# Attention feeding a gated projection, one core: q and k of batches 2 to 7 turned on TensorE instead of by DMA transposes

## The chip, the cores and the metric

The kernel runs on one core of a Trainium2 chip. The metric is the device time of one launch in microseconds (us). Engines are named as in the profile: PE is TensorE (PEld its weight loads), DVE is VectorE, ACT is ScalarE, POOL is GpSimd, and SP is SyncE, which here only issues DMAs.

## What is computed

Attention with a squared ReLU in place of the softmax, for 8 batches of 12 heads, 448 positions and a head size of 64. Then a two-layer projection with a quick GELU:

```python
scores = (1.0 / np.sqrt(D)) * np.matmul(q, k.transpose(0, 1, 3, 2))   # q, k, v: 8, 12, 448, 64
attn = np.maximum(scores, 0.0) ** 2 / S                               # S = 448
x = np.matmul(attn, v).transpose(0, 2, 1, 3).reshape(B * S, H * D)    # 3584, 768
h = x @ w_in                                                          # w_in: 768, 2048
out = (h * (1.0 / (1.0 + np.exp(-1.702 * h)))) @ w_out                # w_out: 2048, 768
```

Inputs and output are float32 in DRAM. The kernel computes in float16 with float32 sums.

## The kernel before, in words

**Units.** The attention is cut into 24 units, three per batch. A unit holds four heads of one batch. Its q (and likewise k and v) is viewed by `quad` (L90) as a tile of 128 partitions, each with two blocks of 448 numbers: a block is one head's seven neighbouring positions times 64. The two blocks on a partition belong to two heads, a = 0 and 1; the two halves of the partitions hold two further heads.

**From DRAM to turned q and k.** The scores need q and k with the head size along the partitions, so each tile is transposed, in 7 column blocks j. Before the change there are three ways.
- Unit 0: SP loads float32 into a staging tile (`load`, L94, tiles kst and qst), DVE casts to float16 (`cast`, L104), and PE transposes (`trans_pe`, L123).
- Units 1 to 5: POOL issues a DMA that casts on the way (`load_cast`, L99), and PE transposes. `trans_pe` makes 14 matmuls of 64 columns each, for two heads and seven blocks, and writes to one PSUM bank ("tr"). `trans_evac` (L133) copies the bank to the tile qT or kT on DVE or ACT.
- Units 6 to 23 (batches 2 to 7): SP loads float32 into the one staging tile, an engine casts it and puts the two heads' columns of a block side by side (`c.rearrange("p j a d -> p a j d")`, L111), and SP issues a DMA transpose into qT or kT (`trans_dma`, L114). PE has no part in it. POOL makes 23 of these casts, ACT 10 and DVE 3.

**Scores and values.** `scores` (L140) makes, for each unit and block j, four matmuls on quarters of the array (64 by 64) into two banks ("sc"). `relu` (L153) and `square` (L162) make the tile "at" on DVE or ACT. `attn_v` (L170) makes 28 quarter-array matmuls of a unit ("av"), and `xt_evac` (L186) copies them to the float16 tile xb.

**The projection.** For batch 0 the first layer is made directly by `m1` (L208, "ht"). For batches 1 to 7 it is made by `unit_product` (L252, "hx"): one level of a Strassen-Winograd scheme with seven products, whose sums of blocks DVE makes. `unit_gelu` and `m1_gelu` run on ACT, and `unit_widen` or `m1_widen` (L204) turn the result to float16 in the tile `ring`, on POOL or DVE. The second layer goes over pairs of 128-row tiles in the same scheme: `pair_product` ("ox"), sums by `a_sum`, and `pair_snap` and `pair_last`, which bring a product to the output tile osb (L82, L366). `store` (L301) issues the output DMAs from SP. The matmuls of all projections are recorded at L194, copies at L78 to L82 and sums at L85.

**What sets the order.** The order of every engine's work is written out by hand as one list of words (from L428). A word names an operation, its unit or tile, the engine after ":" and the PSUM banks after "@"; `tq6@4` would turn q of unit 6 by way of bank 4, `Rq6` does it by DMA transpose, `eq0:a` evacuates on ACT. `Lq`, `Lk` are staged loads, `jq`, `jk`, `V` are casting loads, `Q`, `K` are casts. Each engine runs its operations in that order and waits on semaphores for data and for free buffers. SP's queue thus holds staged loads, DMA transposes and output stores in one line, and POOL's holds casting loads, casts and widenings. A `sp_gate` (L381) makes SP's loads for batch 2 wait until a block of w_in has landed. Buffers that bear on the change: k16 and q16 have 2 each, kT and qT 3, the staging tiles 1; there are 8 PSUM banks.

At the start, 16 matmuls on zeros ("zp") run on PE before data are there.

Of the kernel before, what the change touches and what calls it, by code (L numbers as in the profile page):

```python
# [8 lines left out]
F32 = mybir.dt.float32  # L9
# [6 lines left out]
def kernel(  # L16
# [31 lines left out]
    for name, bufs in (("cst", 1), ("kst", 1), ("qst", 1), ("k16", 2), ("q16", 2), ("v16", 4),  # L48
                       ("kT", 3), ("qT", 3), ("at", 15), ("xb", 2),
                       ("T1", 1), ("T2", 1), ("T4", 1), ("gf", 5),  # L50
                       ("as0", 1), ("as1", 1), ("osb", 3)):
        pool(name, bufs)
# [10 lines left out]
    gate = const("gate", [1, 64])  # L63
# [30 lines left out]
    def load(n, u):  # L94
        x = new(f"{n}st", [128, 2, S], F32)
        nc.sync.dma_start(out=x, in_=quad(n, u))
        units[u][n + "st"] = x

    def load_cast(n, u):  # L99
        x = new(f"{n}16", [128, 2, S], F16)  # L100
        nc.gpsimd.dma_start(out=x, in_=quad(n, u))
        units[u][n + "16"] = x

    def cast(n, e, u):  # L104
        x = units[u].pop(n + "st")
        if u == 0:
            c = new(f"{n}16", [128, 2, S], F16)
            copy(e, c, x)
        else:
            c = new(f"{n}16", [128, J, 2, D], F16)  # L110
            copy(e, c.rearrange("p j a d -> p a j d"), x.rearrange("p a (j d) -> p a j d", d=D))  # L111
        units[u][n + "16"] = c

    def trans_dma(n, u):  # L114
        t = new(f"{n}T", [128, J, 128], F16)
        nc.sync.dma_start_transpose(
            out=t[:, :, :], in_=units[u].pop(n + "16").rearrange("p j a d -> p (j a d)"))
        units[u][n + "T"] = t
# [4 lines left out]
    def trans_pe(n, p, u):  # L123
        ps = bank(p, "tr", F16)
        x = units[u].pop(n + "16")
        for j in range(J):
            for a in range(2):
                nc.tensor.matmul(  # L128
                    out=ps[64 * a:64 * a + 64, j * 128:(j + 1) * 128],
                    lhsT=x[:, a, 64 * j:64 * j + 64], rhs=ident[:, :], is_transpose=True)  # L130
        units[u][n + "ps"] = ps
# [176 lines left out]
    def store_part(e, p, m, h, i):  # L308
# [3 lines left out]
            NOUT + NOUT // 2 * (h - 2), NOUT + NOUT // 2 * (h - 1))  # L312
# [32 lines left out]
    def pair_product(e, p, m, n, h=None):  # L345
        c = (0, 1, 0, 1, 0, 0, 1)[n] if h is None else 2 + h
        if n < 2 or (n == 3 and h is not None):
            op[m, c] = bank(p, "ox")
# [4 lines left out]
        mm(op[m, c][:, k], lambda f: a[:, f, :], lambda f: w[:, f, k], HF, n in (0, 1, 3))  # L353

    def pair_snap(e, p, m, n):
        i, c = {0: (0, lo), 2: (0, hi), 4: (1, hi)}[n]
        copy(e, out_tile(m + i)[:, c], op[m, 0][:, 0:NOUT], 1.0 / SC)

    def pair_last(e, p, m, n, h=None):
        i, c = {1: (0, lo), 3: (1, hi), 5: (1, lo), 6: (0, hi)}[n]  # L360
        o = out_tile(m + i)[:, c][:, quarter(h)]
        if n == 5:
            copy(e, o, op[m, 0][:, 0:NOUT], 1.0 / SC)
        else:
            x = op[m, 1 if h is None else 2 + h][:, quarter(h)]
            nc.vector.scalar_tensor_tensor(out=o, in0=x, scalar=1.0 / SC, in1=o,  # L366
                                           op0=ALU.mult, op1=ALU.add)
# [13 lines left out]
    def sp_gate(e, p, i):  # L381
        nc.sync.dma_start(out=gate[0:1, :], in_=win[i][127:128, 0, 0:64])

    with tc.manual_schedule():
# [4 lines left out]
               "G": sp_gate,  # L389
# [3 lines left out]
        for n in "kq":  # L393
# [3 lines left out]
            two["R" + n] = lambda e, p, u, n=n: trans_dma(n, u)  # L397
# [22 lines left out]
        def zeros(e, p, n):  # L420
# [8 lines left out]
            "z9@0 z1 z1 jq1 z1 z1 jk1 V1 I Lq0 Lk0 z1 z1 z1 Q0:d tq0@1 eq0:a K0:d tk0@2 tq1@3 ek0 "  # L429
            "eq1 s0.5@4.5 jq2 r0.5.1:d r0.5.0 s0.1@6.7 jk2 s0.2@0.1 r0.2.1 r0.1.1:d jq3 s0.0@2.3 "  # L430
            "s0.3@5.4 r0.1.0 r0.2.0:d r0.3.1 r0.3.0:d s0.4@1.7 tk1@6 ek1 s1.6@0.4 s1.4@5.6 jk3 x0.2 "
            "r0.0.0 V0 r0.4.1 r0.0.1 x0.0 r0.4.0 r1.6.0 s0.6@2.7 x0.3 jwa0 s1.0@3.1 r1.6.1 r1.0.1 "
            "tq2@0 x0.5 eq2 s1.5@4.1 r1.4.1 r1.5.0:d s1.3@0.6 jwb0 r1.4.0 r1.5.1 V2 s1.1@4.5 x1.6 "
            "tk2@1 jq4 r1.3.1 jwb2 x1.4 r0.6.1 ek2 r1.1.1 x0.4 jk4 r0.6.0 jwa2 r1.1.0 r1.0.0 tq3@6 "
            "s2.3@7.1 eq3 x0.1 r1.3.0 r2.3.0 s1.2@5.2 r1.2.1 jwa1 x1.1 jwb1 x0.6 tk3@4 r2.3.1 ek3 "
            "jq5 V3 a0@3.6 r1.2.0 jk5 x1.0 jwb3 x1.2 x1.3:a s2.4@0.7 e0.1:a e0.0:a r2.4.0 s3.3@2.1 "
            "x1.5 r3.3.0:d r3.3.1 r2.4.1:d a1@4.5 e1.0:a V4 e1.1:a s2.2@6.3 r2.2.1:d jwa3 s2.5@0.2 "
            "V5 r2.2.0 x2.3 f0.2.0@1 r2.5.0 jo1.0 s2.0@7.4 r2.0.1 s2.1@5.3 r2.1.1 r2.0.0:d r2.5.1 "
            "f0.2.1 jo0.0 x2.2 f0.3.0@6 r2.1.0:d f0.3.1 x2.0 s2.6@0.4 r2.6.1 r2.6.0 s3.1@3.7 r3.1.0 "
            "s3.0@2.5 r3.1.1:d jo1.1 tq4@4 f0.1.0@0 jo0.1 r3.0.0:d eq4 x2.4 x2.6 x2.1:a f0.1.1 "  # L440
            "s3.2@3.7 x2.5:a r3.2.0 a2@2.4 tk4@3 r3.2.1:d r3.0.1 e2.0:a s3.6@7.5 e2.1 ek4 f0.3.2 "
            "r3.6.0:d x3.2 r3.6.1 f0.2.2 g0.3 g0.2 f0.1.2 g0.1 s3.5@2.4 s3.4@3.7 r3.4.0 r3.4.1 "
            "r3.5.0:d s4.4@5.6 r4.4.0:d r4.4.1 v0.2 f0.0.0@1 x3.3 f0.0.1 f0.0.2 f0.8.0@0 g0.0 "
            "s4.5@3.7 r3.5.1:d S0.1 r4.5.0 s4.6@2.5 r4.6.0:d s4.3@6.1 v0.1 f0.8.1 r4.3.0 f0.8.2 "
            "x3.6 r4.6.1 x3.5 x3.0 g0.8 v0.3 s4.2@4.3 r4.2.1 S1.1 s4.1@2.6 r4.2.0 f0.4.0@5 f0.4.1 "
            "f0.5.0@0 f0.4.2 r4.1.0 f0.5.1 x4.6:a x4.2:a G3 v0.8 f0.6.0@3 f0.6.1 r4.3.1:d r4.5.1:d "
            "x3.1 S2.1 f0.6.2 f0.5.2 x4.4 x3.4 f0.7.0@4 g0.6 tq5@2 eq5 S1.2 tk5@1 r4.1.1 g0.4 Lq6 "
            "Lk6 S2.2 ek5:a g0.5 a3@7.3 e3.1:a v0.5 s4.0@2.6 s5.2@5.1 r5.2.1 r4.0.0:d f0.11.0@0 "
            "r4.0.1:d f0.11.1 r5.2.0 f0.11.2 e3.0:a x4.0 x4.5 s5.0@3.1 g0.11 s5.4@2.6 x4.3:a r5.0.1 "
            "s5.5@5.7 f0.7.1 r5.5.1 f0.9.0@0 f0.9.1 f0.9.2 r5.0.0:d f0.7.2 r5.5.0:d s5.3@1.7 r5.4.1 "  # L450
            "x4.1 v0.6 g0.7 a4@3.5 S3.1 s5.1@6.4 r5.3.1 r5.4.0 S2.4 v0.11 v0.7 x5.0:a Q6 r5.3.0:d "
            "s5.6@7.2 S1.3 e4.0 f0.10.0@1 g0.9 S3.2 f0.10.1 v0.9:d r5.6.1 r5.1.1:d u1.2.0@3 S0.3 "
            "f0.15.0@0 x5.3:a f0.14.0@2 r5.1.0 x5.1 f0.15.1 r5.6.0:d v0.4 f0.15.2 f0.14.1 x5.2:a "
            "v0.0 g0.15 f0.10.2 x5.4 T1.1 f0.14.2 u1.3.0@4 g0.10 x5.6:a f0.13.0@6 x5.5 K6 Lk7 "
            "a5@7.0 f0.13.1 S1.4 e4.1:a S3.4 S0.2 S2.3 Lq8 f0.13.2 v0.10:d e5.0:a v0.15:d e5.1:a "
            "Rq6 T1.2 u1.0.0@1 u1.1.0@5 u1.1.1@7 S0.4 t1.0.0 Rk6 g0.14 t1.1.0 T1.3 v0.14:d b1.1.1 "
            "u1.0.2 g0.13 u1.0.1@0 u1.1.2 t1.0.2 u1.0.4 v0.13 b1.0.1 g1.1.1 v1.1.1 W1.1 g1.0.1 "
            "v1.0.1 S3.3 t1.1.2 f0.12.0@2 u1.0.3 t1.0.4 u1.1.4 t1.2.0 T1.4 b1.0.3 u1.1.3 t1.1.4 "
            "u1.3.1@6 g1.0.3 u1.0.6 K7 W2.1 b1.1.3 b1.0.6 u1.0.5 Lk8 f0.12.1 W0.1 v1.0.3 u1.1.6 "
            "u1.2.1@0 g1.0.6 W3.1 b1.1.6 g1.1.3 u1.1.5 b1.2.1 v1.0.6 g1.0.5 u1.2.2 t1.3.0 v1.1.3 "  # L460
            "u1.2.3 g1.2.1 v1.0.5:d v1.2.1 W3.2 t1.2.2 b1.3.1 f0.12.2 W0.2 W0.3 g1.1.6 u1.2.4 g0.12 "
            "p0.0@7 v0.12 t1.2.4 W1.3 Q8:a b1.2.3 v1.1.6 Lq7 u1.2.5 A0.1@0 g1.2.3 W3.3 u1.3.2 Rq8 "
            "A0.2@1 g1.2.5 W2.2 h0.0 u1.2.6 b1.2.6 g1.3.1 v1.3.1 u1.3.3 g1.1.5 W2.4 W1.2 t1.3.2 "
            "p0.1@1 V6 v1.1.5 Rk7 s6.0@2.3 r6.0.0:d A0.3 r6.0.1 v1.2.5 s6.1@0.5 r6.1.0 l0.1 u1.3.4 "
            "t1.3.4 r6.1.1 p0.2 A0.4 x6.0:a s6.2@2.3 r6.2.1 h0.2:d r6.2.0:d s6.4@0.5 r6.4.1 p0.3 "
            "W2.3 b1.3.3 Q7:a W0.4 s6.3@3.2 r6.3.1 x6.1 p0.4 W1.4 K8:p r6.4.0 r6.3.0 W3.4 h0.4 "
            "x6.3:a Rq7 Lk9 l0.3 Lq9 x6.4 u1.3.5 s6.5@5.2 s6.6@0.3 r6.6.1 g1.3.5 r6.6.0 x6.2 u1.3.6 "
            "r6.5.1:d p0.5 r6.5.0 b1.3.6 g1.2.6 s7.0@3.4 l0.5 v1.2.6 r7.0.0:d x6.5 r7.0.1 x7.0 "
            "s7.2@0.2 r7.2.1 s7.4@5.6 r7.4.1 p0.6 s7.1@7.3 s7.6@4.2 r7.4.0 V8 V7 v1.3.5 r7.1.0:d "
            "Rk8 x7.4 x6.6:a r7.1.1 a6@6.5 r7.6.0 s7.3@7.3 K9:p l0.6 Q9 r7.6.1 e6.0:a r7.3.0:d "  # L470
            "r7.3.1 s7.5@4.1 r7.5.0 Lk11 e6.1 p2.0@2 x7.6 r7.2.0 Rk9 s8.5@6.7 s8.4@3.4 x7.1 "
            "s8.2@5.0 r7.5.1 r8.5.1 r8.2.1 Rq9 p2.1@1 A2.1@1 s8.1@7.0 r8.2.0:d r8.4.1 r8.4.0 x7.2 "
            "x7.3 r8.5.0 r8.1.0:d K11:p s8.3@5.4 r8.1.1 x7.5:a r8.3.0 Rk11 r8.3.1:d x8.1:a a7@3.6 "
# [151 lines left out]
```

## Time and profile before

| | us |
|---|---|
| median of 3 runs | 362.71 |
| lowest and highest | 362.51, 363.19 |
| profiled execution, its own time | 363.36 |
| span of its instructions | 361.6 |
| PE, DVE, ACT, POOL busy | 351.8, 313.2, 286.0, 116.9 |

The span is the time from the first to the last instruction in the profile. An engine's busy time is the part of it in which one of its instructions was running. In a row of the profile, "out<-in" names the tile written and those read, "xN" is the number of instructions, and a number such as L194 is the line of the kernel. In the chain of waits each piece has its start, its length and what it was.

### The profile page before, as it was taken

The numbers are of one execution on the slowest core, as the hardware profiler recorded it, in microseconds if no ns is written. First come the engines' busy times: TensorE is split into PE (matmuls) and PEld (weight loads), VectorE is DVE, ScalarE is ACT, GpSimd is POOL, SyncE is SP. The second block draws the span as 40 slices with busy tenths as digits, with TensorE's granted clock in tenths as the row PEclk, the third lists the DMA queues.
The fourth block names the chain that finished last, engine by engine and source line by source line (L and its number), as shares of the span: only waits on it lengthen the run. The fifth ranks groups of instructions, "written<-read, shape, count | busy, mean of one in ns | idle before, by whom it ended". The sixth has DMA issues, their size and how long they took to land.

```text
span 361.6 us, 9118 instructions
## 1 busy us (share of the span) xinstructions
PE 351.8 (97%) x3600; PEld 240.6 (67%) x3600; DVE 313.2 (87%) x578; ACT 286.0 (79%) x551; POOL 116.9 (32%) x169
## 2 busy tenths in 40 slices
PE   8799999999999999999999999999999999999995
PEld 4444458854579655896568865698579756778663
DVE  3999999999998899899988898989998898674844
ACT  3999898999988998789997799868987898427410
POOL 5735731435135424242244343254121310102000
PEclk9999999999999999999999999999999999999999
DMA  8999999679889999868699625980381101130314
GB/s 178 159 195 205 217 234 240 126 122 229 189 224 268 210 164 182 204 121 199 145 195 172 198 33 86 210 200 0 68 175 46 44 2 45 45 87 2 87 45 133
DMA packets 65388, 51.39 MB, mean 142 GB/s; under 512 B 35776, under 2 KB 62016, under 8 KB 65344
## 3 DMA queue, kind: packets, MB, share of 16 engines
q1 hardware_dynamic: 48336, 36.32, 43.0%
q0 software_dynamic: 16608, 14.09, 26.7%
q8 instruction: 28, 0.46, 0.5%
q10 hardware_dynamic: 400, 0.39, 0.3%
q14 instruction: 16, 0.13, 0.1%
HBM read 45.61 MB, written 11.01 MB: 157 GB/s over the span
## 4 chain that ended last, share of the span: by engine, by line
PE 85%; DMA 6%; DVE 4%; ACT 2%; POOL 2%; issue 1%; POOLq 0%
PE ox L194 34%; PE hx L194 32%; PE sc L147 8%; PE av L178 7%; DMA k<-in_k_dram 3%; DMA q<-in_q_dram 3%; PE ht L214 3%; PE zp L424 1%; DVE at L85 1%; DVE at L158 1%; POOL ring L204 1%; ACT at L160 1%; ACT gf L201 1%; PE tr L128 0%; DVE asum L85 0%
## 5 line engine op out<-in xcount | busy, mean ns | idle before, releaser
L160 ACT ACTIVATE at<-sc 128x448 f16<-128x448 f32 x214 | 104.9, 582 | 7.3 <-PE sc L147 7.2
L204 POOL TENSOR_SCALAR ring<-gf 128x448 f16<-128x448 f32 x94 | 58.0, 617 | 156.1 <-ACT gf L201 152.7
L194 PE MATMUL ox<-wout,ring 128*128 128x384 f16 (+1 forms) x456 | 80.3, 324 | 0.1
L194 PEld LDWEIGHTS <-ring 128*128 128x128 f16 x568 | 53.7, 98 | 35.9 <-issue 6.1
L158 DVE TENSOR_SCALAR at<-sc 128x448 f16<-128x448 f32 x122 | 72.2, 616 | 3.6 <-PE sc L147 2.7
L194 PEld LDWEIGHTS <-win 128*128 128x128 f16 x672 | 64.0, 98 | 6.6 <-issue 3.0
L85 DVE TENSOR_TENSOR at<-at 128x896 f16<-128x896 f16 x102 | 63.1, 644 | 0.3
L166 ACT ACTIVATE at<-at 128x896 f16<-128x896 f16 x66 | 62.7, 969 | 0.8 <-DVE at L158 0.5
L85 DVE TENSOR_TENSOR gf<-hx,gf 128x448 f32<-128x448 f32 x84 | 51.1, 620 | 10.8 <-PE hx L194 4.9
L201 ACT ACTIVATE gf<-gf 128x448 f32<-128x448 f32 x84 | 46.8, 573 | 15.1 <-DVE gf L85 14.9
L194 PE MATMUL hx<-xb,win 128*128 128x224 f16 x504 | 58.0, 259 | 0.0
L147 PE MATMUL sc<-qT,kT 64*64 64x448 f16 x672 | 49.7, 358 | 2.0 <-DVE kT L80 1.4
L194 PEld LDWEIGHTS <-winS 128*128 128x128 f16 x504 | 48.2, 98 | 2.7 <-issue 1.1
L76 ACT ACTIVATE gf<-hx 128x448 f32<-128x448 f32 x59 | 31.4, 542 | 13.2 <-PE hx L194 9.5
L194 PE MATMUL ox<-wT,asum 128*128 128x384 f16 (+1 forms) x232 | 41.0, 321 | 0.7 <-DVE osb L366 0.5
L194 PE MATMUL hx<-T,winS 128*128 128x224 f16 x336 | 39.7, 259 | 0.0
L178 PE MATMUL av<-at,v 64*64 64x448 f16 x672 | 37.1, 350 | 1.2 <-ACT at L160 0.7
L147 PEld LDWEIGHTS <-kT 64*64 64x64 f16 x672 | 18.0, 105 | 25.9 <-issue 18.8
L194 PEld LDWEIGHTS <-asum 128*128 128x128 f16 x232 | 21.4, 98 | 16.8 <-issue 4.4
L366 DVE SCALAR_TENSOR_TENSOR osb<-ox,osb 128x384 f32<-128x384 f32 (+1 forms) x44 | 23.3, 533 | 8.9 <-PE ox L194 6.9
L178 PEld LDWEIGHTS <-v 64*64 64x64 f16 x672 | 19.8, 106 | 14.0 <-issue 2.8
L80 POOL CAST q<-qst 128x896 f16<-128x896 f32 x13 | 13.4, 1028 | 39.6 <-DMA qT<-q 14.5
(57 smaller groups left out, 363.3 us busy)
## 6 DMA issues: line engine op xcount, KB each, us to landing
out_dram<-osb SPq DMA_DIRECT2D x52, 192.0 KB, 3.4
qst<-in_q_dram SPq DMA_DIRECT2D x19, 448.0 KB, 4.9
kst<-in_k_dram SPq DMA_DIRECT2D x19, 448.0 KB, 4.4
v<-in_v_dram POOLq DMA_DIRECT2D x24, 224.0 KB, 5.7
win<-in_moe_w_in_dram POOLq DMA_DIRECT2D x8, 384.0 KB, 12.3
wout<-in_moe_w_out_dram POOLq DMA_DIRECT2D x4, 768.0 KB, 20.6
q<-in_q_dram POOLq DMA_DIRECT2D x5, 224.0 KB, 5.3
k<-in_k_dram POOLq DMA_DIRECT2D x5, 224.0 KB, 5.9
```

The lines of the kernel that those rows point to most:

```text
L76: nc.scalar.activation(out=o, in_=i, func=AF.Copy)
L80: eng[e].tensor_copy(out=o, in_=i)
L85: eng[e].tensor_tensor(out=o, in0=x, in1=y, op=op)
L147: nc.tensor.matmul(out=sc[a][c, 0:S], lhsT=st["kT"][r, j, c], rhs=st["qT"][r, :, c], start=True, stop=True)
L158: nc.vector.tensor_scalar(out=o, in0=i, scalar1=0.0, scalar2=None, op0=ALU.max)
L160: nc.scalar.activation(out=o, in_=i, func=AF.Relu)
L166: nc.scalar.activation(out=at, in_=at, func=AF.Square)
L178: nc.tensor.matmul(out=av[s][64 * a:64 * a + 64, 0:S], lhsT=v16[r, a, 64 * j:64 * j + 64], rhs=at[r, a, :], start=(j == 0), stop=(j == J - 1))
L194: nc.tensor.matmul(out=o, lhsT=lhs(i), rhs=rhs(i), start=start and i == 0, stop=i == n - 1, skip_group_check=True)
L201: nc.scalar.activation(out=o, in_=i, func=AF.Gelu_apprx_sigmoid, scale=1.0 / SC)
L204: eng[e].tensor_scalar(out=o, in0=i, scalar1=SC, scalar2=1.0, op0=ALU.mult, op1=ALU.mult)
L366: nc.vector.scalar_tensor_tensor(out=o, in0=x, scalar=1.0 / SC, in1=o, op0=ALU.mult, op1=ALU.add)
```

## The change

- `load_cast` gets a second form for q and k of units 6 to 23: two casting DMAs from POOL, one for each head a. Each writes pieces of 64 numbers so that the two heads' columns of a block j lie side by side.
- `trans_pe` gets a second form for tiles laid out so: 7 matmuls of 128 columns on the whole array instead of 14 of 64.
- `trans_dma` and the gate are gone, and `cast` keeps only the side-by-side layout, which unit 0 now has too. Units 6 to 23 have no staged load and no cast on an engine.
- k16 and q16 have 4 buffers each instead of 2. The staging tiles are gone; unit 0 is staged in `ring`, which is unused at that time.
- The second layer's copies to osb may come in another order (`from_bank`): the first to come is copied, the second added. The last pair's halves are cut differently.
- The whole list of words is new. The shares of DVE, ACT and POOL in operations that may run on either are new too.

```diff
-    for name, bufs in (("cst", 1), ("kst", 1), ("qst", 1), ("k16", 2), ("q16", 2), ("v16", 4),
+    for name, bufs in (("cst", 1), ("k16", 4), ("q16", 4), ("v16", 4),
...
     def load(n, u):
-        x = new(f"{n}st", [128, 2, S], F32)
-        nc.sync.dma_start(out=x, in_=quad(n, u))
-        units[u][n + "st"] = x
+        o = "kq".index(n) * 4 * S
+        x = ring.rearrange("p f c -> p (f c)")[:, o:o + 4 * S].bitcast(F32)
+        units[u][n + "st"] = x.rearrange("p (a c) -> p a c", a=2)
+        nc.sync.dma_start(out=units[u][n + "st"], in_=quad(n, u))
 
     def load_cast(n, u):
-        x = new(f"{n}16", [128, 2, S], F16)
-        nc.gpsimd.dma_start(out=x, in_=quad(n, u))
+        if n == "v" or u < 2 * NP:
+            x = new(f"{n}16", [128, 2, S], F16)
+            nc.gpsimd.dma_start(out=x, in_=quad(n, u))
+        else:
+            x = new(f"{n}16", [128, J, 2, D], F16)
+            for a in range(2):
+                nc.gpsimd.dma_start(
+                    out=x[:, :, a, :], in_=quad(n, u)[:, a, :].rearrange("p (j d) -> p j d", d=D))
+            x = x.rearrange("p j a d -> p (j a d)")
         units[u][n + "16"] = x
...
-    def trans_dma(n, u):
-        t = new(f"{n}T", [128, J, 128], F16)
-        nc.sync.dma_start_transpose(
-            out=t[:, :, :], in_=units[u].pop(n + "16").rearrange("p j a d -> p (j a d)"))
-        units[u][n + "T"] = t
...
         for j in range(J):
+            if len(x.shape) == 2:
+                nc.tensor.matmul(out=ps[:, j * 128:(j + 1) * 128],
+                                 lhsT=x[:, j * 128:(j + 1) * 128], rhs=ident[:, :],
+                                 is_transpose=True)
+                continue
             for a in range(2):
...
+    def from_bank(e, x, t, c):
+        o = out_tile(t)[:, c]
+        part_done = (t, c.start) in begun
+        begun.update((t, i) for i in range(c.start, c.stop, NOUT // 2))
+        if part_done:
+            nc.vector.scalar_tensor_tensor(out=o, in0=x, scalar=1.0 / SC, in1=o,
+                                           op0=ALU.mult, op1=ALU.add)
+        else:
+            copy(e, o, x, 1.0 / SC)
...
-    def sp_gate(e, p, i):
-        nc.sync.dma_start(out=gate[0:1, :], in_=win[i][127:128, 0, 0:64])
```

A stretch of the list, for units 17 to 21, before and after:

```diff
-            "x17.0 r18.0.0 K20:p Lq21 s17.5@5.7 r17.5.1 h14.0:d s17.1@3.6 Rq20 A14.2@1 r17.1.0:d "
-            "p12.6 x18.2:a p14.1@0 Rk23 p14.2 Lk22 o13 l12.6 r17.5.0 r17.1.1 x17.1:a x17.4 "
...
+            "r17.3.1 x17.2 r17.3.0 tk23@1 l12.6 p14.1@4 ek23:a x17.3 o12 x18.6:a tq20@5 s18.5@7.2 "
...
+            "p14.2 r18.0.1 e17.0 r18.0.0 e17.1 r18.4.1 s19.4@1.7 T5.1 s19.5@0.2 r19.4.0 tq21@6 T5.3 "
+            "r19.5.0 u5.0.0@5 T5.2 tk20@1 r19.5.1:d t5.0.0 u5.1.0@0 r19.4.1 x19.5 u5.0.1@2 eq21:a "
```

## The prediction

> **What bounds the kernel now.** I read the page's busy shares first, then the windows, then the chain that ended last. On the page TensorE (PE) is busy nearly all the time:
>
> ```profile
> PE 351.8 (97%) x3600; PEld 240.6 (67%) x3600; DVE 313.2 (87%) x578; ACT 286.0 (79%) x551; POOL 116.9 (32%) x169
> PEclk9999999999999999999999999999999999999999
> ```
>
> A busy PE is not a PE at its peak, since the ends of its records are modelled. So I ask what its stream must take. The chain of waits (start, length, what; all in us) gives the rates, a piece ending where the next begins:
>
> ```profile
> 50.52 2.65 PE ht L214 x14
> 54.12 1.45 PE av L178 x28
> 131.93 1.32 PE av L178 x28
> 133.63 6.61 PE ox L194 x40
> 140.24 0.50 PE sc L147 x8
> 157.03 7.01 PE hx L194 x72
> 164.04 0.69 PE sc L147 x12
> 242.32 8.05 PE hx L194 x84
> 338.94 18.25 PE ox L194 x128
> ```
>
> hx takes 8.05/84 = 0.0958 a matmul, ht 2.65/14 = 0.189, av 1.32/28 = 0.047. Twelve sc cost 0.19 more than eight: 0.047 each. Eight at that rate are 0.38 and show 0.50, so going from quarter-array sc to a full-array stream costs about 0.1. The 40 ox before an sc block give (6.61 - 0.1)/40 = 0.163; of the last 128, 32 are 192 columns wide, at 0.083. A transposition at L128 is 14 half-array matmuls:
>
> ```profile
> 17.12 0.58 PE L128 MATMUL tr<-ident,k 128*64 128x128 f16 x14
> L128 PE MATMUL tr<-ident,k x84: 217/219/243, 7.0 to 39.9; 128*64 128x128 f16 x84
> ```
>
> From the timeline's 0.58 I take the last record's 0.219: 0.36 for 13 steps, 0.028 a step, so 0.39 for 14. The records start in pairs, a pair every 0.055: two halves side by side.
>
> The sum over counts from the program: ox 768 x 0.1625 = 124.8, narrow ox 32 x 0.083 = 2.7, hx 1176 x 0.0958 = 112.7, ht 96 x 0.189 = 18.1, sc and av 672 each x 0.047 = 63.2, 12 transpositions 4.7, zp 5.3: **331.5**. The order of instructions changes the array's shape 125 times: 125 x 0.1 = 12.5. PE starts at 1.1, and 4.4 remain after its last matmul starts. These make 349.5 of 361.6; **12.1 are waits of PE**. Most are early. The sixth av block ends at 55.2; the stream up to it is 43.2, plus 34 changes (3.4) and the start of 1.1: 47.7. So 7.5 of the 12.1 lie before 55.2, and only 4.6 behind it. The windows (length, then busy time of each engine, clock, DMA share, GB/s) show why:
>
> ```profile
> 0.00:20.00 20.00, 16.14 (x224) 8.90 (x224) 13.91 (x28) 13.73 (x29) 12.13 (x22) 1.00 0.99 171
> 20.00:40.00 20.00, 19.82 (x238) 9.81 (x230) 19.55 (x38) 18.10 (x37) 11.12 (x13) 1.00 1.25 202
> 180.00:200.00 20.00, 20.00 (x202) 14.52 (x195) 17.18 (x32) 17.11 (x30) 7.52 (x10) 1.00 1.05 180
> 280.00:300.00 20.00, 20.00 (x201) 12.88 (x200) 17.93 (x33) 17.96 (x38) 4.51 (x8) 1.00 0.09 22
> ```
>
> At the start PE waits for first data and for VectorE and ScalarE (DVE, ACT), which turn scores into squares; from about 60 on PE is never free. The DMA share is high in one late window and near nothing in the other, with PE at 20.00 in both: **relieving DMA cannot shorten that stretch**.
>
> **The change, part by part.**
>
> *PE gains work.* 36 DMA transposes become 36 PE transpositions of 7 full-array matmuls; q and k of unit 0 go from 14 half-array to 7 full ones. A full one streams 128 columns, as a half one does, and a pair of halves takes 0.055, so I price 7 at 0.39, the row nearest in kind. 36 x 0.39 = **+14.1**; unit 0 saves nothing. Low end: if a full one took a single half's step, 0.028, 7 cost 0.20 and the sum is +7.1. High end: if the 128-column weight load were not hidden, its record of 0.098 (page, L194) would set the step: 0.69 each, +24.7. For the row: hx steps of 0.0958 already include such a load.
>
> The Trainium skill speaks against my price ("TensorE: Matmul & The Clock Gate", Back-to-back issue gap): a sustained stream of loads and matmuls at 128 columns runs at about 81 ns a matmul. By that the term would be 36 x 7 x 0.081 = 20.4, 6.3 more; no full-array transposition is in this trace, while the half-array pairs, which load as many columns, ran at 55 ns.
>
> *Order.* Shape changes go from 125 to 134: **+0.9**. Products, scores and attention matmuls keep their number.
>
> *DVE and ACT.* 36 evacuations of 128x896 come in, 18 on each:
>
> ```profile
> L80 DVE COPY kT<-tr 128x896 f16<-128x896 f16 x5 | 3.1, 621 | 1.3 <-PE tr L128 1.3
> L76 ACT ACTIVATE kT<-tr 128x896 f16<-128x896 f16 x1 | 0.9, 938 | 0.0
> ```
>
> DVE: 18 x 0.62 = +11.2. The new order also moves to it 14 xb copies (+8.7), 13 widenings from POOL (+5.5), 8 squares (+5.0), 7 osb copies (+3.9) and small ones (+0.4); it gives up 16 relus (-9.5), 4 hx copies (-2.4), 4 casts (-2.5). Net +20, to about 333. ACT: +16.7 of evacuations, +7.8 relus, +2.1 hx copies, against -8.5 casts, -7.6 squares, -7.8 xb, -3.4 osb: about even, 285. Over a span near 375 these are 89% and 76%, as 87% and 79% now. So I cost them at nothing beside PE; the cover is PE's own stream. If it is gone (attention stretches, where DVE is fullest), half of the added 20 on the path would cost up to 10.
>
> *POOL.* 23 casts go (-24.4), 13 widenings (-8.0). 72 DMA issues of 896 pieces come; wout, 1024 pieces, took 0.878 each, so 72 x 0.85 = +61. POOL goes to about 146, 39%: hidden. Widenings and v loads stand behind these issues, and an issue waits until a buffer of q16/k16 is turned; four buffers instead of two, and loads ordered several units ahead, make me cost this at nothing. Uncovered, a widening held up delays the sums and products behind it; as an outer price I keep POOL's longest single wait now, 18.9 (for ACT gf), inside the bounds on waits below.
>
> *SP and DMA.* SP loses 38 loads but for unit 0's two, 36 transposes and the gate; only stores remain, so they can only start earlier. DMA packets:
>
> ```profile
> q1 hardware_dynamic: 48336, 36.32, 43.0%
> q0 software_dynamic: 16608, 14.09, 26.7%
> ```
>
> From the trace's packets by size, the loads through kst and qst (9,728 packets) took 60 us of all 16 engines and the transposes (32,256 of 256 B) 57; both go but for unit 0's two loads. In come 36 x 1792 = 64,512 packets of 128 B written, read from 256 B. Casting packets took 79 ns for 768 B and 98 for 1024 B; along that line 128 B is 30, an estimate, and 64,512 x 30/16 = 121: even. High end: 79 as for 768 B, 318; low end: 18 ns, the transposes' median, 73. I take 30, since the 256 B packets averaged 28.
>
> The Trainium skill warns here too ("DMA: Bandwidth & Descriptors", Why small descriptors are slow): a fixed cost per packet weighs more on small ones, with about 27% lost at 256 B. That would make the 121 some 154, still under the span; no 128 B packet is in this trace.
>
> *What stalls go or stay.* The first 55 us still run units 0 to 5 on PE transposes, with the same relus and squares. More q16/k16 buffers let loads start without waiting for a turn (POOL waited 3.3 and 1.5 for PE tr): perhaps 1 to 2 less. Each new transposition holds a PSUM bank from its first matmul to the end of its evacuation, which only the early stretch knew; 36 of them may add some waits of 0.1 to 0.2, up to 7. I take waits of 11 in all (bounds 5 and 20).
>
> **Sum.** 331.5 + 14.1 + 134 x 0.1 + 5.5 = 364.5 with no wait at all; with 11 the span is 375.5. The profiled execution took 363.36, 1.76 outside its span: 377.3. The shown median, 362.71, is 0.65 below it: **376.6**.
>
> **Rivals.**
> 1. *DMA becomes the bound.* v, weights, stores and the first loads take about 130 us of the 16 engines, and loads must be in by about 320, before the last scores. So small packets may cost up to (320 - 130) x 16/64,512 = 47 ns before they bind. At 65 they need 262: the span is about 392 + 10 at the end, and the time some **400**. For it: the share is over 1 in several windows; against: 28 ns at 256 B. Chance 0.08.
> 2. *The weight load is not hidden in full-array transpositions:* 24.7 instead of 14.1, **387**. For it: nothing else alternates a load with so short a matmul on the full array. Chance 0.08.
> 3. *Faster: the transpositions fit into PE's waits.* Place: the waits of 12.1. Price: 0.20 each (0.028 a matmul), 7.1, and all waits gone: 361.6 + 7.1 + 0.9 - 12.1 = 357.5, time **358.6**. It decides from 36 transpositions and changes under 11.4, that is 0.29 each. Against: 7.5 of the waits are early, where no new transposition is needed yet, and 128 columns have never streamed through all rows and columns in less than hx's rate, 0.055. Chance 0.03; about no change, 0.02.
> 4. *The change doesn't do what it says* (half-array turns remain, 14 per tile): the price per tile is the same 0.39 and the time too, so it has no number of its own; the order shows 266 full matmuls.
>
> The forecast holds 0.79, mostly 370 to 384: waits of 5 to 18. With the load-bound case and some of the rest the range is 368.5 to 388. Measurements of this kernel tell about 0.2% from no change; faster by that 0.03, within 0.02, slower 0.95.
>
> **What would show it.** Right: a tr group of full-array matmuls starting 0.055 apart, PE streams near 346, late windows still at 20.00 busy, waits under 5 after the first 60. Wrong: tr steps near 0.1 (rival 2); PE idle with DMA landing of q or k as releaser (rival 1); DVE kT or qT as releasers of sc for over 5 in all; a first stage over by 50 instead of 55.

## The result, and the profile after

The changed kernel takes 391.19 us (median of 3 runs, 390.33 to 391.63) against 362.71: a ratio of 1.0779 with a 95% interval of 1.0745 to 1.0812. The sign was foretold and the size was not: the forecast was 376.6, the range ended at 388. The profiled execution took 390.33, its span 388.6.

The page after, in the order in which the page before was read: busy shares, granted clock, the DMA row of the 40 slices, and the two large DMA queues.

```profile
PE 369.8 (95%) x3830; PEld 254.8 (66%) x3830; DVE 325.5 (84%) x614; ACT 287.9 (74%) x551; POOL 156.7 (40%) x205
...
PEclk9999959999999999999999999999999999999999
DMA  9999999828995889961399910930041401111045
...
q0 software_dynamic: 82272, 22.36, 58.2%
q1 hardware_dynamic: 5104, 11.54, 10.8%
```

PE's share fell from 97% to 95% although it has more to do, and one slice of the clock row shows a 5: in the sixth of 40 slices, about 49 to 58 us, PE was granted about half its full clock. The loads of q and k have gone from the hardware queue, q1, to POOL's, q0, and the DMA row shows 9, a share of 0.9 or more, in its first seven slices, to 68 us. The windows put numbers on the place:

```profile
20.00:40.00 20.00, 19.84 (x243) 9.85 (x243) 19.43 (x38) 18.98 (x39) 10.00 (x13) 1.00 1.48 196
40.00:60.00 20.00, 10.27 (x67) 4.21 (x60) 8.89 (x19) 7.38 (x16) 12.67 (x15) 0.74 1.53 194
180.00:200.00 20.00, 20.00 (x208) 13.89 (x207) 16.79 (x32) 16.80 (x34) 8.13 (x10) 1.00 0.32 21
```

The windows from 20 to 40 and from 180 to 200 show PE as before (19.84 and 20.00 busy), the late one with a DMA share of 0.32 instead of 1.05. Between 40 and 60 PE is busy 10.27 of 20 at a mean clock of 0.74, and DVE and ACT are idle for more than half of it; DMA is not, and POOL less so. The stretch from 36 to 70, before and after:

```profile
36.00:70.00 34.00, 33.57 (x346) 23.32 (x344) 33.02 (x62) 30.55 (x57) 15.96 (x22) 1.00 1.15 209
36.00:70.00 34.00, 21.93 (x172) 10.29 (x170) 18.43 (x37) 18.33 (x36) 20.82 (x25) 0.85 1.75 183
```

PE was busy 33.57 of 34 and is busy 21.93 now. So most of the loss lies in one place. The page's waits name its links (engine and what waited, releaser: total, times, longest):

```profile
POOL q L106 <- PE tr L125: 22.2, 5, 7.2
...
ACT gf L203 <- POOL ring L206: 16.7, 7, 10.9
...
PE sc L149 <- ACT gf L203: 9.7, 1, 9.7
```

PE waits 9.7 in one piece for ACT, and ACT 10.9 in one piece for POOL's widening into `ring`. Before, ACT's gelus waited 2.7 for POOL in all. The first line is the largest, but costs nothing by itself: a kernel below (ten widenings on DVE) has 22.3 of it and no pause. What kept POOL shows in the chain that ended last, here between 35 and 67 us, where the third of the late widenings (63.40) holds PE:

```profile
35.06 11.27 DMA wout<-in_moe_w_out_dram
...
46.61 15.44 DMA wout<-in_moe_w_out_dram
...
62.34 0.98 POOL q L106
...
63.40 0.61 POOL ring L206
...
64.03 0.55 ACT gf L203
...
64.63 1.51 PE av L180 x26
...
66.81 0.39 PE tr L125 x7
```

Read it backwards. PE's av waits for a gelu, the gelu for a widening, the widening stands in POOL's queue behind a q load, and the q load waits until a block of w_out has landed that it does not read. In the trace POOL's transfers carry eight semaphores in turn (numbers 99 to 106), and an issue waits on its own, that is until the transfer eight before it has landed. From the issue at 35.06 to that at 46.61, and from there to the one at 62.34, it is eight transfers each time. The stretch of POOL's timeline in which the first widening is late (start, length, what; in brackets the idle time before it and its releaser):

```profile
41.16 3.91 POOL L106 DMA_DIRECT2D k<-in_k_dram  x4
46.61 0.90 POOL L387 DMA_DIRECT2D wout<-in_moe_w_out_dram  x1 [1.54 <-DMA wout<-in_moe_w_out_dram]
48.03 0.96 POOL L106 DMA_DIRECT2D q<-in_q_dram  x1 [0.52 <-DMA v<-in_v_dram]
51.62 0.98 POOL L106 DMA_DIRECT2D q<-in_q_dram  x1 [2.63 <-DMA wout<-in_moe_w_out_dram]
52.68 0.56 POOL L206 TENSOR_SCALAR ring<-gf 128x448 f16<-128x448 f32 x1
```

Before, the fourth w_out issue stood at 37.00 and the first four widenings began at 37.95, since q and k went through SP's queue. Now six casting issues for k and q and the last block of w_out stand between w_out's third block and the widening, which comes at 52.68. ACT waits for it from 42.42 on. Until 52.68 POOL is idle for 1.54, 0.52 and 2.63, together 4.7, because a transfer has not landed; in nearly all the rest, about 5.5, it makes the issues themselves. The timeline of ACT and PE goes on from there:

```profile
53.28 0.54 ACT L203 ACTIVATE gf<-ht 128x448 f32<-128x448 f32 x1 [10.86 <-POOL ring L206]
53.87 1.45 PE L149 MATMUL sc<-qT,kT 64*64 64x448 f16 x7 [9.73 <-ACT gf L203]
55.26 6.33 PE L216 MATMUL ht<-xb,win 128*128 128x448 f16 x22
```

22 ht at 0.189 are 4.16; here they take 6.33, while the granted clock from 53.87 to 61.50 is 0.64. The pause costs its 9.7, then 2.2 on the ht, and up to 1.1 on the seven sc (1.45 instead of 0.33). The third late widening adds a wait of 2.35 before av.

### The profile page after: what moved, and what is told of

The parts are those of the page before. It is cut to its first block, busy times and chain, and to the rows that moved or that the text cites. A ratio compares the mean times of both kernels' runs of the same rounds, so it can differ in the third digit from the quotient of the medians.

```text
span 388.6 us, 9528 instructions
## 1 busy us (share of the span) xinstructions
PE 369.8 (95%) x3830; PEld 254.8 (66%) x3830; DVE 325.5 (84%) x614; ACT 287.9 (74%) x551; POOL 156.7 (40%) x205
## 4 chain that ended last, share of the span: by engine, by line
PE 83%; DMA 14%; ACT 1%; POOL 1%; issue 1%; DVE 0%; SPq 0%
PE ox L196 34%; PE hx L196 29%; PE sc L149 8%; PE av L180 7%; DMA wout<-in_moe_w_out_dram 7%; PE tr L125 4%; DMA v<-in_v_dram 3%; DMA q<-in_q_dram 3%; DMA ring<-in_k_dram 1%; PE ht L216 1%; ACT at L162 0%; POOL q L106 0%; ACT k L75 0%; DVE kT L79 0%; POOL ring L206 0%
## 5 line engine op out<-in xcount | busy, mean ns | idle before, releaser
L162 ACT ACTIVATE at<-sc 128x448 f16<-128x448 f32 x230 | 112.2, 563 | 7.3 <-PE sc L149 6.9
L206 POOL TENSOR_SCALAR ring<-gf 128x448 f16<-128x448 f32 x81 | 50.9, 628 | 143.5 <-ACT gf L203 125.8
L196 PE MATMUL ox<-wout,ring 128*128 128x384 f16 x448 | 80.7, 326 | 0.0
L160 DVE TENSOR_SCALAR at<-sc 128x448 f16<-128x448 f32 x106 | 62.9, 617 | 18.0 <-PE sc L149 17.2
L84 DVE TENSOR_TENSOR at<-at 128x896 f16<-128x896 f16 x110 | 67.5, 635 | 3.1 <-ACT at L162 2.3
L149 PE MATMUL sc<-qT,kT 64*64 64x448 f16 x672 | 52.2, 361 | 10.5 <-ACT gf L203 9.7
L168 ACT ACTIVATE at<-at 128x896 f16<-128x896 f16 x58 | 56.0, 967 | 3.1 <-DVE at L160 2.9
L106 POOL DMA_DIRECT2D q<-in_q_dram x36 | 35.8, 994 | 29.6 <-PE tr L125 22.2
L75 ACT ACTIVATE gf<-hx 128x448 f32<-128x448 f32 x63 | 33.4, 545 | 13.4 <-PE hx L196 10.9
L196 PE MATMUL ox<-wT,asum 128*128 128x384 f16 x224 | 40.8, 327 | 0.0
L106 POOL DMA_DIRECT2D k<-in_k_dram x36 | 35.5, 987 | 7.1 <-PE tr L125 4.3
```

The source lines that it names most:

```text
L75: nc.scalar.activation(out=o, in_=i, func=AF.Copy)
L84: eng[e].tensor_tensor(out=o, in0=x, in1=y, op=op)
L106: nc.gpsimd.dma_start(out=x[:, :, a, :], in_=quad(n, u)[:, a, :].rearrange("p (j d) -> p j d", d=D))
L149: nc.tensor.matmul(out=sc[a][c, 0:S], lhsT=st["kT"][r, j, c], rhs=st["qT"][r, :, c], start=True, stop=True)
L160: nc.vector.tensor_scalar(out=o, in0=i, scalar1=0.0, scalar2=None, op0=ALU.max)
L162: nc.scalar.activation(out=o, in_=i, func=AF.Relu)
```

## The experiments

Each was timed with the kernel before on the same chip (363.12 for the first four, 363.04 for the others). The theory: POOL's widenings of batch 0, held in line behind load issues, stop ACT and then PE. The main rivals: data of q and k late for PE itself; a dearer transposition; the packets of 128 B.

**The three widenings to DVE.** Only the engine of three words is another.

```diff
-  r3.6.0:d v0.3 s4.1@7.0      S0.1 v0.2 f0.6.1      r4.6.0:d v0.0 s5.0@2.0
+  r3.6.0:d v0.3:d s4.1@7.0    S0.1 v0.2:d f0.6.1    r4.6.0:d v0.0:d s5.0@2.0
```

> The changed kernel with three early widenings of batch 0 (v0.3, v0.2, v0.0) made by DVE instead of POOL; loads, transpositions and all else as they are. Theory Q (a widening stands in POOL's queue behind casting loads that wait for room among eight DMAs in flight, so ACT gets no free gf buffer, and relus and scores stop): the PE gap of about 10 us near 44 to 54 goes, and most of the half-clock stretch behind it; 376 to 381. Rival D (DMA is full until about 69 us and PE waits for data that land late, whatever POOL's queue does): 387 to 391. Rival P (the PE transpositions and the new order themselves are dearer than priced): no change, 390 to 391.

Measured: 386.32, ratio 1.0646 (1.0621 to 1.067). The first pause is gone: the sixth av block ends at 56.7 instead of 71.7. (Such an end is, here and in the prediction, the start of the block's last matmul.) But the next widening that is still on POOL, v0.14, meets the same line. The timeline of this kernel:

```profile
64.74 0.56 POOL L206 TENSOR_SCALAR ring<-gf 128x448 f16<-128x448 f32 x1
65.33 0.54 ACT L75 ACTIVATE gf<-hx 128x448 f32<-128x448 f32 x1 [10.53 <-POOL ring L206]
...
66.36 3.52 PE L196 MATMUL hx<-xb,win 128*128 128x224 f16 x18 [8.67 <-ACT gf L203]
```

The mechanism is shown, the gain I expected was not reached: the widening that is late moved by 12 us (52.68 to 64.74), and PE's wait shrank by one (9.73 to 8.67).

**The loads later.** Eight load words (jk7, jk6, jq7, jk8, jk9, jq9, V8, V10) go behind v0.0; the widenings stay on POOL.

```diff
-  f0.1.0@6 x2.2 jk7 r3.2.1 ... S1.2 r4.2.1 r4.6.0:d v0.0 s5.0@2.0 r4.2.0
+  f0.1.0@6 x2.2 r3.2.1 ... S1.2 r4.2.1 r4.6.0:d v0.0 jk7 jk6 jq7 jk8 jk9 jq9 V8 V10 s5.0@2.0 r4.2.0
```

> The changed kernel with the casting loads jk7, jk6, jq7, jk8, jk9, jq9 and the v loads V8 and V10 moved behind the widening v0.0 in the list, otherwise the same. Theory Q: v0.3, v0.2 and v0.0 get through behind wout alone, so the early gap shrinks to a few us: 377 to 382. Rival D: the same bytes in the same full queue, and those of batch 2 later still: 388 to 396. Rival P: no change.

Measured: 387.29, ratio 1.0669 (1.0647 to 1.0691). The three widenings now start between 41.94 and 43.22, so the loads were what held them; v0.14 is held instead, until 65.88, and PE waits 6.2 for ACT there. It is the same result from the other side.

**Every full-array transposition twice.** 252 more matmuls of 128 columns, to the same result.

```diff
-            if len(x.shape) == 2:
+            for _ in range(2 if u >= 2 * NP else 1 if len(x.shape) == 2 else 0):
                 nc.tensor.matmul(out=ps[:, j * 128:(j + 1) * 128],
...
-                continue
+            if len(x.shape) == 2:
+                continue
```

> The changed kernel with every transposition of units 6 to 23 made twice into the same bank (252 full-array matmuls more, the same result). If PE is bound wherever they stand and a matmul takes 0.056: 252 x 0.056 = 14.1 more, 404 to 406. If the weight load sets the step (0.098): 414 to 417. If transpositions fit into idle time of PE: under 395.

Measured: 403.72, ratio 1.113 (1.1099 to 1.116), so 12.5 above the changed kernel: 12.5/252 = 0.050 each. That is near the predicted 0.056; the 0.028 and 0.098 of its two ends fall.

**Plain loads and half-array turns throughout.** One DMA per tile, in pieces of 896 B, and 14 half-array matmuls, as units 1 to 5 have it.

```diff
-        if n == "v" or u < 2 * NP:
+        if True:
```

> The changed kernel with q and k of units 6 to 23 loaded as units 1 to 5 are: one casting DMA a tile in plain layout, 256 packets of 896 B, and turned by 14 half-array matmuls. 36 POOL issues and 55,296 packets fewer. Theory Q: eight DMAs in flight then hold twice as many tiles and POOL's queue stops less early: 376 to 384, with up to 7 of that taken back by more changes of the array's shape (36 x 2 x 0.1). Rival D: DMA time falls by 57 against 23 us x (36 tiles)/16 in shares, so the full stretch ends some 8 us earlier: 380 to 386. Rival P (full-array turning): the same 390 as half-array turning has the same price, or more by the shape changes: 391 to 398.

Measured: 386.92, ratio 1.0673 (1.0632 to 1.0714). With 36 issues fewer POOL is 110.3 busy instead of 156.7, its first widening comes at 42.75, and the sixth av block ends at 61.5, 10.3 earlier. Only 4.3 of that is left at the end. Each half-array turn between full-array matmuls brings up to two changes of shape; 36 x 2 x 0.1 = 7.2 would be enough for the rest, but I only worked that out.

**Ten widenings to DVE:** all eight of batch 0 that were POOL's, and the first two of batch 1.

```diff
-  v0.3  v0.2  v0.0  v0.14  v0.4  v0.12  v0.13  v1.0.1  v1.1.1  v0.9
+  v0.3:d  v0.2:d  v0.0:d  v0.14:d  v0.4:d  v0.12:d  v0.13:d  v1.0.1:d  v1.1.1:d  v0.9:d
```

> The changed kernel with all eight of POOL's widenings of batch 0 and the first two of batch 1 made by DVE; loads unchanged. Theory Q, as the first runs left it (the gap went to the next POOL widening behind the loads): with none left before about 66 us, neither gap shows, nor the half clock behind it: 374 to 378. Rival D (loads land late because DMA is full): the gap stays somewhere else before 70 us, 384 to 388. Rival B (the free time gets eaten by a DVE that now has ten more instructions of 0.31): 380 to 384.

Measured: **376.54** (376.23 to 377.08), ratio 1.0381 (1.0359 to 1.0403). No pause is left. The windows of this kernel, in the two places that were short:

```profile
40.00:60.00 20.00, 19.57 (x200) 11.26 (x189) 19.55 (x43) 16.91 (x36) 12.24 (x14) 1.00 1.53 194
60.00:80.00 20.00, 18.90 (x184) 15.43 (x183) 18.32 (x39) 15.94 (x32) 15.53 (x20) 1.00 1.56 132
```

The DMA share is that of the changed kernel (1.53 in the same window), the packets and PE's instructions are the same, and the load issues keep their order. So neither late data nor the price of packets or matmuls made the 14.6 us; the place of ten small POOL instructions behind load issues did. Of the 28.5 that the change costs, 12.5 are the turns, going by their doubling, and a little over 1 is left that no run divides.

**The three to DVE, and five loads later.** As the first, with jk8, jk9, jq9, V8 and V10 moved behind v1.1.1.

```diff
-  tq8@4 v1.1.1 t1.0.2
+  tq8@4 v1.1.1 jk8 jk9 jq9 V8 V10 t1.0.2
```

> The changed kernel with v0.3, v0.2 and v0.0 on DVE, and the casting loads jk8, jk9, jq9, V8 and V10 moved behind the widening v1.1.1; POOL keeps all other widenings. Theory Q: fewer loads stand before v0.14 and its followers, so most of the second gap goes as well without taking work from POOL: 375 to 380. Rival D: the later loads come late for their units, 384 to 390.

Measured: 384.1, ratio 1.0587 (1.0569 to 1.0604). Now v0.14 is in time and the widening behind the moved loads is late. POOL's and ACT's timeline of this kernel:

```profile
64.21 3.94 POOL L106 DMA_DIRECT2D k<-in_k_dram  x4
68.15 1.95 POOL L106 DMA_DIRECT2D q<-in_q_dram  x2
70.09 1.47 POOL L102 DMA_DIRECT2D v<-in_v_dram  x2
71.65 0.55 POOL L206 TENSOR_SCALAR ring<-gf 128x448 f16<-128x448 f32 x1
...
72.24 0.54 ACT L75 ACTIVATE gf<-hx 128x448 f32<-128x448 f32 x1 [7.51 <-POOL ring L206]
```

These eight issues stand without idle time between them; they take 7.4 one after another, and ACT waits 7.51. So there are two holds: an issue that waits for the transfer eight before it, and the issues' own time in a block. The first pause of the changed kernel had both, 4.7 and about 5.5.

**The ten to DVE and the five loads later**, the edits of the last two together.

> Both edits: ten early widenings on DVE, and the five loads behind v1.1.1. Theory Q: 373 to 378, near the sum without any wait of 364.5 plus 1.1 and waits of 8 to 12. Rival D: as the loads-later run, 384 to 390.

Measured: 377.17, ratio 1.0392 (1.0368 to 1.0417), the same as without the later loads. With those ten off POOL, the place of the five loads made no difference.

**The transpositions alone, in the order of before.** Staged loads, casts and list as before; each DMA transpose is replaced, at its place or up to 44 words later, by 7 full-array matmuls with the evacuation directly behind them.

```diff
-  Rq6 T1.2 u1.0.0@1 u1.1.0@5 u1.1.1@7 S0.4 t1.0.0 Rk6 g0.14
+  T1.2 u1.0.0@1 tq6@0 eq6:a u1.1.0@5 u1.1.1@7 S0.4 t1.0.0 tk6@0 ek6:d g0.14
```

> The kernel before, with its order, its staged loads and its casts on engines, in which each DMA transpose is replaced, at its place in the list or up to 44 words later, where a PSUM bank is free, by 7 full-array matmuls and an evacuation on DVE and ACT in turn. PE's part of the change alone: 36 x 0.39 = 14.1 on a PE that is full, so 376 to 380, with up to 4 more for waits on banks. If PE's transpositions were hidden: under 366. If the new order and loads have no part in the 28 us: 388 or more.

Measured: 402.51, ratio 1.1086 (1.106 to 1.1112), far above what I expected. One row of the waits of this kernel:

```profile
DVE qT L80 <- PE tr L128: 11.3, 9, 3.3
```

An evacuation that stands right behind its turn in the list makes DVE or ACT wait for PE (31.4 in 28 waits over all of them), and what is queued behind it comes late for PE, which falls to 16.07 busy from 80 to 100 and 15.65 from 140 to 160. So this run says nothing on the price of the turn. It suggests that an order must set turn and evacuation apart, as the new list does; no run has the order of before with the two apart.

No version beat the kernel before. With no wait at all the predicted sum, an estimate, is a span of 364.5, above the 361.6 of before.

## Why the prediction was wrong in size, step by step

- **PE's stream, right.** A turn is 0.39 in most pieces of the chain, as priced, and doubling it gave 0.050 a matmul. The Trainium skill's rule ("TensorE: Matmul & The Clock Gate", Back-to-back issue gap), about 81 ns a matmul, does not hold for these: they start 56 ns apart.
- **The late stretch, right.** The "waits" of the prediction are what its sum leaves over of a span, not waits read from the trace; PE's idle time by its records was 9.8 before, 18.8 after and 8.1 with ten widenings on DVE. Of the 24.1 us left over (388.6 - 364.5), 22.2 lie before the end of the sixth av block (71.7, against a stream of 44.9 + 3.5 for changes + 1.1 = 49.5) and 1.9 behind it. Before they were 7.5 and 4.6. The up to 7 for PSUM banks did not come.
- **DVE and ACT, near.** 325.5 and 287.9 busy against 333 and 285.
- **Packets, right.** 64,512 packets of 128 B took 32.7 ns on the mean (30 estimated), 132 us of the 16 engines (121). The estimate of 154 by the Trainium skill's "DMA: Bandwidth & Descriptors", Why small descriptors are slow, was too high: it put the page's 27% on top of a figure taken from measured packets, which hold their overhead already.
- **POOL's issues, low.** 0.98 to 0.99 each instead of 0.85: 71 for the 72, not 61. POOL's 156.7 against 146 would still be hidden by share.
- **The step that failed:** "Widenings and v loads stand behind these issues, and an issue waits until a buffer of q16/k16 is turned; four buffers instead of two, and loads ordered several units ahead, make me cost this at nothing". The buffers were the wrong thing to look at. The issues wait for the transfer eight before them and take 0.98 each, and the widenings wait in line with them: one came 10.9 late for ACT, and PE stood for 9.7. Even the k load at 55.72, whose wait the profile puts down to PE, started 0.5 after the third block of w_out, eight transfers before it, had landed (55.18). I judged POOL and DMA by their shares of the whole span (39%; 121 us of packets), where the first 68 us decide: there the DMA share is 0.9 or more in every slice, w_in, w_out and the loads share one queue, and ACT needs a widening soon. I named the price if uncovered, 18.9, but put it "inside the bounds on waits" of 5 to 20 and took 11; it belongs on top. Moving the ten widenings takes 14.6 off and gives 376.54, with 374.5 - 364.5 = 10 left over: the sum and the 11 fit a kernel without this pause. That 376.54 meets the forecast of 376.6 so closely is partly luck: by doubling, the turns cost 12.5 and not 14.1, and the 10 left over, for which 11 were taken, was not measured term by term.
- **"The first 55 us ... perhaps 1 to 2 less"** fell with it: the stage ended at 71.7, and even without the pause at 56.1 (ten widenings on DVE) against 55.2.
- **Rivals.** DMA as the bound: its share was high, but only early, and none of the waits of PE that the profile lists for the changed kernel ends with a DMA; the path ran through POOL's queue. The dear weight load and the gain on PE's waits: refuted by doubling.

What stays open: how the 4.7 us that POOL waited in the first hold divide between the turn of eight and transfers that would have landed late anyway. No run had another number of transfers in flight with the same bytes.

## What to carry to other kernels

When loads move onto an engine's queue, list what else is in that queue and who needs it soonest; an engine that is 40% busy can still stop the whole kernel with one instruction that is ten us late. Judge a transfer queue in the stretch where it is busiest, not by its share of the span. A price found for "if the cover is gone" is a case of its own and goes on top of the usual waits, not into their range.

## What the runs showed of the hardware that I had not expected

- A POOL transfer's issue waits, in these programs, for the one eight before it. Two blocks of w_out landed 11.27 and 15.44 us after their issue, and the issue eight behind each could not start before; POOL's idle time just ahead of them was 1.54 and 0.95.
- A casting issue of 896 pieces of 128 B takes 0.98 us on POOL, one of 256 pieces of 896 B 0.72, and w_out's of 1024 pieces 0.89.
- With a pause of 9.7 us on PE the granted clock was 0.74 in that 20 us window, and 22 ht matmuls took 6.33 us instead of 4.16; without the pause (ten widenings on DVE) it was 1.00 there.
- Small packets keep the engines busy for fewer bytes: a packet of 128 B took 32.7 ns on the mean, one of 768 B 79. From 36 to 70 us DMA moved 183 GB/s at a share of 1.75, where the kernel before moved 209 at 1.15.
